# Linear attention into a feed-forward layer: stepping the state every 64 tokens, with block-diagonal k^T and scaled q^T from one crossbar transpose

## The chip, the cores and the metric

One core of one Trainium2 chip runs the whole program. The metric is device time in microseconds (us), one launch, median over several executions. Each execution carries a state. "Slow" means here that it took over 1.5% longer than the fastest of the same kernel; verdicts use the fast ones. Engine names: TensorE (PE in profiles; PEld is its weight load), VectorE (DVE), ScalarE (ACT), GpSimd (POOL), SyncE (SP; its DMA queue is SPq). In the text, "crossbar transpose" is a DMA transpose from on-chip memory to on-chip memory, and "software queue" is the DMA queue that GpSimd issues.

## The reference

Linear attention with a decay per head (4 sequences, 8 heads, 768 tokens, head size 64), then a feed-forward layer of 512 to 2048 to 512 over the 3072 tokens:

```python
for b in range(nb):                      # blocks of 64 tokens
    intra = einsum('bhic,bhjc->bhij', qb, kb) * Dmask      # lam^(i-j), i >= j
    intra = einsum('bhij,bhjd->bhid', intra, vb)
    inter = einsum('bhid,bhde->bhie', qb * lam_pow, kv_state)
    out[:, :, sl] = intra + inter
    kv_state = lam_block * kv_state + einsum('bhsd,bhse->bhde', kb * rev_pow, vb)
...
h = x @ w_in
g = where(h >= 1, h, where(h <= -1, 0, (h + 1)**2 / 4))    # SmeLU
return g @ w_out
```

Inputs and output are float32; the kernel computes in bfloat16 with float32 sums.

## The kernel before

It works in chunks of 128 tokens, 24 in all, 6 per sequence. The decays are moved into tables: v is multiplied by lam^-n, q by lam^n, so no mask with powers is needed and the state is a plain sum. All engines run from one static plan: a small planner in the kernel gives every operation an assumed duration and orders each engine's instructions by it. An engine executes its list in that order.

Chunks 0 to 3 ("plain") transpose k and q on TensorE. From chunk 4 on, k^T lies block-diagonally (two heads on 128 partitions), in two halves g of 64 tokens; the queries of the first half meet only the first half's keys, those of the second half meet both:

```python
def f_xt(c):                              # from chunk 8: crossbar; chunks 4 to 7 use TensorE
    nc.sync.dma_start_transpose(out=t..., in_=qk[c]...)          # 8 blocks of 128x128: k and q
def cast_v(c):
    nc.gpsimd.tensor_tensor(vn, qkv_ld[c, 2], tab_k, op=mult)    # one multiply, 128x512
def f_vb(c, g, hi):                       # 4 small copies per chunk, by DMA, into block-diagonal v
    nc.gpsimd.dma_start(out=vi[HD[hi], :, g, hi, :], in_=vn[HD[g], :, hi, :])
def f_kb(c, hi):                          # block-diagonal k^T, two DVE copies
    nc.vector.tensor_copy(kbd[HD[hi], :, :, hi, :], ptt[c][HD[hi], 0]...)
def f_qT(c):
    nc.vector.tensor_tensor(qT[c], ptt[c][:, 1], tab_q, op=mult)
def f_u(c):                               # state update, 4 matmuls of 128 columns per chunk
    ...
def f_s(c, g):                            # scores: 4 of 128 columns (g=0), 4 of 64 (g=1)
    nc.tensor.matmul(pst[c, g][:, hp, :], lhsT=kbd[:, hp, g], rhs=qT[c][:, hp, 64 * g:])
def f_o(c):                               # output: per pair of heads, state then values
    for hp in range(HP):
        nc.tensor.matmul(po[:, hp], lhsT=ubd[...], rhs=qT[c][:, hp, :])               # 128 columns
        for g in range(2):
            nc.tensor.matmul(po[:, hp, 64 * g:], lhsT=vi[:, hp, g], rhs=sc_sb[c][g])  # 128, 64
# ... feed-forward: L1 into ph, ACT relu -> r, DVE t, w, gT, L2 into py
```

The feed-forward work of DVE is three operations per group: t = min(r/2, 1), w = r - t, gT = w * t, 48 of each.

## Time and profile before

| | before |
|---|---|
| time, median of 3 (range) | 221.22 us (220.75 to 221.24) |
| span of the profiled execution | 220.2 us |
| busy: TensorE, DVE, ACT, GpSimd | 96%, 70%, 62%, 47% |
| first second-layer matmul starts | 35.9 us |
| last weight block landed | 48.1 us |

A busy share says only that an engine had something to do.

### The profile page before, as it was taken

To read this page: it belongs to the slowest core of one execution; us is meant where nothing else is said; L and a number is where in the kernel's file an instruction comes from. 1 tells how busy PE (TensorE), PEld (TensorE's weight loads), DVE (VectorE), ACT (ScalarE), POOL (GpSimd) and SP (SyncE) were. 2 spreads that over 40 slices of the span, in tenths; PEclk is the share of its full clock that TensorE was granted. 3 is DMA by queue.
4 is the path that set the end of the run, shared out by engine and by line. 5 is a ranking of instruction groups with operands and counts; after the bars stand their busy time and mean duration, and the time that the engine had idled before them with its cause. 6 is when DMAs were issued, how large, how long until landed. Compare 5 with 4: busy or idle time off the path is not lost.

```text
span 220.2 us, 5365 instructions
## 1 busy us (share of the span) xinstructions
PE 210.5 (96%) x2147; PEld 152.2 (69%) x2180; DVE 154.8 (70%) x276; ACT 136.2 (62%) x249; POOL 103.7 (47%) x143
## 2 busy tenths in 40 slices
PE   7897999989999999999999999999999999999993
PEld 2566788866787858978877677767677776766441
DVE  6543888999499695998999887687668657364200
ACT  6766685655689558677867667755755753554121
POOL 8999874972588545746664357336060000000000
PEclk9999999999999999999999999999999999999999
DMA  5999999959999999989878895796533110110112
GB/s 139 237 239 234 264 209 233 191 98 249 252 245 206 254 226 272 196 223 228 166 186 210 208 209 141 185 212 166 148 75 99 48 47 3 48 48 33 67 57 86
DMA packets 83945, 36.54 MB, mean 166 GB/s; under 512 B 74256, under 2 KB 78352, under 8 KB 83920
## 3 DMA queue, kind: packets, MB, share of 16 engines
q1 hardware_dynamic: 75472, 24.39, 47.6%
q0 software_dynamic: 8304, 11.80, 23.8%
q8 instruction: 17, 0.28, 0.5%
q14 instruction: 8, 0.07, 0.1%
q10 hardware_dynamic: 144, 0.00, 0.0%
HBM read 27.27 MB, written 6.29 MB: 152 GB/s over the span
## 4 chain that ended last, share of the span: by engine, by line
PE 81%; DVE 8%; POOL 5%; DMA 4%; issue 1%; ACT 0%; POOLq 0%; ACTq 0%
PE py L386 35%; PE ph L347 34%; DMA w_in_sb<-in_moe_w_in_dram 4%; PE ps L306 3%; PE po L330 3%; DVE w L365 2%; PE po L324 2%; PE pu L294 2%; DVE gT L380 2%; DVE t L361 2%; POOL x2f L428 1%; POOL vn L262 1%; PE pt L275 1%; DVE sc L317 1%; POOL x1f L428 1%
## 5 line engine op out<-in xcount | busy, mean ns | idle before, releaser
L347 PE MATMUL ph<-xT,w_in_sb 128*128 128x128 bf16 (+1 forms) x1152 | 98.9, 237 | 1.1 <-DMA w_in_sb<-in_moe_w_in_dram 1.1
L355 ACT ACTIVATE r<-ph,one 128x512 bf16<-128x512 f32 x96 | 65.6, 687 | 53.0 <-PE ph L347 41.1
L386 PE MATMUL py<-w_out_sb,gT 128*128 128x512 bf16 x354 | 90.0, 379 | 1.5
L347 PEld LDWEIGHTS <-w_in_sb 128*128 128x128 bf16 x1152 | 80.5, 98 | 12.4 <-DMA w_in_sb<-in_moe_w_in_dram 1.3
L386 PEld LDWEIGHTS <-gT 128*128 128x128 bf16 x384 | 35.8, 98 | 28.7
L269 POOL DMA_DIRECT2D vi<-vn x80 | 50.2, 644 | 10.2 <-POOL vn L262 6.2
L262 POOL TENSOR_TENSOR vn<-x2f,tab_k 128x512 bf16<-128x512 f32 x24 | 27.4, 1140 | 46.0 <-DMA x2f<-in_v_dram 33.2
L361 DVE TENSOR_SCALAR t<-r 128x1024 bf16<-128x1024 bf16 x48 | 27.5, 572 | 28.6 <-ACT r L355 28.6
L365 DVE TENSOR_TENSOR w<-r,t 128x1024 bf16<-128x1024 bf16 x48 | 36.9, 769 | 1.2
L380 DVE TENSOR_TENSOR gT<-w,t 128x1024 bf16<-128x1024 bf16 x48 | 35.3, 735 | 0.9
L317 DVE TENSOR_TENSOR sc<-ps,causal 128x512 bf16<-128x512 f32 (+1 forms) x40 | 22.1, 553 | 5.7 <-PE ps L306 5.4
L391 ACT COPY osb<-py 128x512 f32<-128x512 f32 x24 | 14.1, 586 | 13.9 <-PE py L386 13.1
L337 ACT CAST xT<-po 128x512 bf16<-128x512 f32 x24 | 14.0, 584 | 9.1 <-PE po L330 7.6
L298 ACT CAST ubd<-pu 64x256 bf16<-64x256 f32 x40 | 14.6, 364 | 1.6 <-PE pu L294 1.4
L306 PEld LDWEIGHTS <-kbd 128*128 128x128 bf16 x160 | 10.8, 98 | 6.9 <-issue 0.9
L252 ACT CAST qk<-x0f 128x512 bf16<-128x512 f32 x23 | 14.1, 615 | 0.7 <-DMA x0f<-in_q_dram 0.6
L306 PE MATMUL ps<-qT,kbd 128*128 128x128 bf16 (+1 forms) x160 | 13.3, 206 | 1.0 <-DVE qT L288 0.8
L252 ACT CAST qk<-x1f 128x512 bf16<-128x512 f32 x23 | 14.1, 613 | 0.0
L324 PE MATMUL po<-qT,ubd 128*128 128x128 bf16 x80 | 13.6, 221 | 0.0
L330 PE MATMUL po<-sc,vi 128*128 128x128 bf16 (+1 forms) x160 | 12.9, 206 | 0.0
L229 PE MATMUL py<-idle 128*128 128x512 bf16 x33 | 10.8, 464 | 1.5 <-DVE one L117 1.2
L330 PEld LDWEIGHTS <-vi 128*128 128x128 bf16 x160 | 11.1, 98 | 1.4
(50 smaller groups left out, 122.9 us busy)
## 6 DMA issues: line engine op xcount, KB each, us to landing
out_dram<-osb SPq DMA_DIRECT2D x24, 256.0 KB, 2.2
x1f<-in_k_dram SPq DMA_DIRECT2D x18, 256.0 KB, 3.8
x0f<-in_q_dram SPq DMA_DIRECT2D x18, 256.0 KB, 4.2
x2f<-in_v_dram SPq DMA_DIRECT2D x17, 256.0 KB, 4.5
vi<-vn POOLq DMA_DIRECT2D x80, 32.0 KB, 3.6
w_in_sb<-in_moe_w_in_dram POOLq DMA_DIRECT2D x4, 512.0 KB, 8.3
w_out_sb<-in_moe_w_out_dram POOLq DMA_DIRECT2D x4, 512.0 KB, 9.5
x2f<-in_v_dram POOLq DMA_DIRECT2D x7, 256.0 KB, 4.9
```

Source lines behind the costliest of these rows:

```text
L252: nc.scalar.copy(out=t, in_=qkv_ld[c, x])
L262: nc.gpsimd.tensor_tensor(vn[c % NV].rearrange("p a b d -> p (a b) d"), qkv_ld[c, 2], _bc(tab_k[:, c % NCB, :], 2, D), op=AX.mult)
L269: (nc.gpsimd if c < VP else nc.sync).dma_start(out=o, in_=i)
L306: nc.tensor.matmul(pst[c, g][:, hp, :], lhsT=kbd[c % NKB][:, hp, g].rearrange("p a d -> p (a d)"), rhs=qT[c][:, hp, 64 * g:], start=True, ...
L317: nc.vector.tensor_tensor(sc_sb[c][g], pst[c, g], _bc(causal[:, 0:128 - 64 * g], 1, HP), op=AX.mult)
L330: nc.tensor.matmul(po[:, hp, 64 * g:], lhsT=vi[c % NV][:, hp, g].rearrange("p a d -> p (a d)"), rhs=sc_sb[c][g][:, hp, :], start=(cb == 0 ...
L347: nc.tensor.matmul(ph[:, j * m:(j + 1) * m], lhsT=w_in_sb[:, ko, (i + j) * 128:(i + j + 1) * 128], rhs=xT[s][:, ko, p * m:(p + 1) * m], st ...
L355: nc.scalar.activation(out=r_t[grp][:, i, :], in_=ph_t[s, ni, part], func=AF.Relu, bias=one[:, 0:1])
L361: nc.vector.tensor_scalar(t_t[grp], r_t[grp], 0.5, 1.0, op0=AX.mult, op1=AX.min)
L365: nc.vector.tensor_tensor(w_t[grp], r_t[grp], t_t[grp], op=AX.subtract)
L380: nc.vector.tensor_tensor(o, w, t, op=AX.mult)
L386: nc.tensor.matmul(py_t[s, ms], lhsT=gT[s][:, ko, ms * 128:(ms + 1) * 128], rhs=w_out_sb[:, ko, :], start=(ko == 0), stop=(ko == FO - 1))
```

## The change

Its intent: make chunks of 64 tokens, from chunk 4 on, out of each 128. Then no query meets another half's keys, scores and values need only 64-column matmuls, and the state steps in between. The block structure is made before the transpose: four casts of k, each of a quarter (64 partitions, 256 elements), write to other partitions than they read and lay k block-diagonally; q is scaled in its cast; one crossbar transpose of 12 blocks then yields both. TensorE's transposes of chunks 4 to 7 go. The DMA copies of v become GpSimd operations: four quarter multiplies and two copies per chunk. In chunks 1 to 3 the order of the output matmuls changes.

```diff
+    LD, RING, VBN, VCN = 6, 6, 620, 600       # planner's durations of the new GpSimd work
+    KE = ('ACT', 'DVE', 'ACT', 'DVE')         # engines of the four k casts
+    def f_ki(c, g, hi):
+        o, i = kq[c % NKQ][HD[hi], HP * g:HP * g + HP, HD[hi]], quarter(qkv_ld[c, 1], g, hi)
+        if KE[2 * g + hi] == "ACT":
+            nc.scalar.copy(out=o, in_=i)
+        else:
+            nc.vector.tensor_tensor(o, i, i, op=AX.max)
+    def f_qn(c):
+        nc.vector.tensor_tensor(kq[c % NKQ][:, 2 * HP:, :]..., qkv_ld[c, 0], tab_n..., op=AX.mult)
     def f_xt(c):
-        ...  in_=qk[c]                        # 8 blocks, chunks 8 to 23
+        nc.sync.dma_start_transpose(out=t, in_=kq[c % NKQ]...)     # 12 blocks, chunks 4 to 23
+    # cast_v, from chunk 4: four quarters with another output partition
+            nc.gpsimd.tensor_tensor(vn[c % NV][HD[hi], HP * g:HP * g + HP, :], quarter(qkv_ld[c, 2], g, hi), ...)
-        (nc.gpsimd if c < VP else nc.sync).dma_start(out=o, in_=i)
+        nc.gpsimd.tensor_copy(vi[c % NV][HD[hi], :, HD[hi]], vn[c % NV][HD[hi]])
     def f_s(c, g):                            # 8 matmuls of 64 columns per chunk
+                for j in range(2):
+                    nc.tensor.matmul(t[:, hp, HD[j]], lhsT=kT[c][:, HP * j + hp, :], rhs=qT[c][:, hp, HD[j]], ...)
     def f_o(c):
+        if c < PLAIN:                         # chunks 0 to 3: the state matmuls first, then the values
+            ...
+        for j in range(2):
+            for hp in range(HP):
+                if cb > 0 or j > 0:
+                    nc.tensor.matmul(po[:, hp, HD[j]], lhsT=ubd[(2 * c + j - 1) % NUB][:, hp, :], rhs=qT[c][:, hp, HD[j]], ...)
+                nc.tensor.matmul(po[:, hp, HD[j]], lhsT=vi[c % NV][:, HP * j + hp, :], rhs=sc_sb[c, 1][:, hp, HD[j]], ...)
 # ... buffers, loads (chunk 6 to the SyncE queue), planner entries cut
```

## The prediction

> **What bounds the kernel now.** I read the page's busy table and slices first, then the chain that ended last, then TensorE's timeline, and last the DVE and GpSimd timelines where TensorE stood still.
>
> ```profile
> span 220.2 us, 5365 instructions
> ...
> PE 210.5 (96%) x2147; PEld 152.2 (69%) x2180; DVE 154.8 (70%) x276; ACT 136.2 (62%) x249; POOL 103.7 (47%) x143
> ...
> PE   7897999989999999999999999999999999999993
> ...
> PEclk9999999999999999999999999999999999999999
> ...
> PE 81%; DVE 8%; POOL 5%; DMA 4%; issue 1%; ACT 0%; POOLq 0%; ACTq 0%
> ```
>
> The fourth line is the busy share of TensorE in 40 slices of 5.5 us: below 9 only in the first four slices, in slice 9 (44 to 49.5 us), and at the end. The clock is full. 81% of the last chain (last line) is TensorE. But busy time is not peak, so I checked the spacing of starts:
>
> ```profile
> 111.85 0.28 PE L306 MATMUL ps<-qT,kbd 128*128 128x64 bf16 x4
> 111.97 1.04 PE L347 MATMUL ph<-xT,w_in_sb 128*128 128x256 bf16 x8
> 112.84 0.39 PE L294 MATMUL pu<-vn,qk 128*128 128x128 bf16 x4
> 113.07 1.03 PE L386 MATMUL py<-w_out_sb,gT 128*128 128x512 bf16 x4
> 113.93 0.22 PE L324 MATMUL po<-qT,ubd 128*128 128x128 bf16 x1
> 113.98 0.25 PE L330 MATMUL po<-sc,vi 128*128 128x128 bf16 x2
> ...
> 114.49 1.04 PE L347 MATMUL ph<-xT,w_in_sb 128*128 128x256 bf16 x8
> ```
>
> Each row is start, duration, what, how many; a group lasts until the next group's start. Four 64-column matmuls take 0.12 us (30 ns each), eight of 256 columns 0.87 (109 ns), four of 512 0.86 (215 ns), and four triples of 128, 128 and 64 columns (113.93 to 114.49) 0.56, so 56 + 56 + 28 ns. Nothing stands between them. So from about 34 us the time is a sum over columns: a matmul removed there comes off the end, if nothing else stalls. The one large stall is this, and the two rows after it (DVE) tell why:
>
> ```profile
> 48.81 0.38 PE L306 MATMUL ps<-qT,kbd 128*128 128x128 bf16 x4 [0.84 <-DVE qT L288]
> ...
> 40.01 1.83 DVE L361 TENSOR_SCALAR t<-r 128x1024 bf16<-128x1024 bf16 x1
> ...
> 43.66 2.35 DVE L365 TENSOR_TENSOR w<-r,t 128x1024 bf16<-128x1024 bf16 x1
> ```
>
> These DVE operations otherwise take 0.42 and 0.69 us. GpSimd's multiply for v ran at 40.47 and 44.39 us, within both.
>
> **What the Trainium skill says.** (1) "TensorE: Matmul & The Clock Gate", section "Wait — 56ns, not 53.3ns?": start to start N/2.4 GHz plus about 2.5 ns, 55.6 ns at 128 columns, with a floor of about 25 ns. For 64 columns that makes 29 ns, above the floor; the trace agrees (30 and 56). (2) The same page, "Back-to-back issue gap", gives about 81 ns at 128 columns in a real stream with weight loads; the trace does not agree (56 ns, with a load before each), and I take the trace. This matters: if weight loads bound, splitting 128 columns into two 64s would gain nothing. (3) "SBUF — State Buffer", section "SBUF: two separate sides": GpSimd and VectorE share a port pair, locked for a whole instruction, when DVE runs a two-port mode or has two SBUF inputs. The 1.83 and 2.35 us above agree. (4) "DMA: Bandwidth & Descriptors", "DMA Transpose (X-bar)", lets the transpose run from the Sync queue only in 2-byte types; the trace has 16 of them there. No figure is taken from it.
>
> **The change, part by part.** Counts are from the instruction lists of the two builds; prices 29 ns (64 columns) and 56 ns (128). TensorE, chunks 4 to 23:
>
> - PE transposes of chunks 4 to 7 go to the crossbar: 32 x 56 = -1.79 us.
> - Scores: 80 of 128 and 80 of 64 (6.80 us) become 160 of 64 (4.64): -2.16. The block-diagonal k of 64 tokens only meets its own 64 queries.
> - Scores times v, the same counts: -2.16.
> - State times q: 68 of 128 (3.81) become 148 of 64 (4.29), since also the first block of a sequence has a half with a past: +0.48.
> - State update: 64 of 128 (3.58) become 12 of 128 and 132 of 64 (4.50): +0.92, as the state also steps in mid chunk.
>
> Sum -4.71 us. All of it lies after 34 us, on the path.
>
> In chunks 1 to 3 the output matmuls are reordered: state matmuls first, then the half-width ones, where before they alternated. Alternating is dear: in chunk 3, starts run from 32.06 to 33.41 us, 1.35 us for 12 matmuls, while chunk 0, with eight half-width ones alone, needs 0.35. After: 4 x 56 + 350 + about 100 for one switch = 0.67. So -0.7 per chunk. Chunk 3 is on the path; chunk 2 gates the next first-layer group through its eviction, so I count it too; chunk 1 is swallowed by the wait for the second weight block (1.12 us at 19.63). One more filler matmul is planned after chunk 3: +0.2. Net -1.2.
>
> TensorE in all: -4.7 - 1.2 = -5.9 us.
>
> Other engines, by these rows (count, busy us, mean ns, idle):
>
> ```profile
> L269 POOL DMA_DIRECT2D vi<-vn x80 | 50.2, 644 | 10.2 <-POOL vn L262 6.2 <-issue 2.0 <-PE po L330 1.0
> L262 POOL TENSOR_TENSOR vn<-x2f,tab_k 128x512 bf16<-128x512 f32 x24 | 27.4, 1140 | 46.0 <-DMA x2f<-in_v_dram 33.2 <-PE ph L347 6.4 <-PE ps L306 6.4
> L298 ACT CAST ubd<-pu 64x256 bf16<-64x256 f32 x40 | 14.6, 364 | 1.6 <-PE pu L294 1.4
> L252 ACT CAST qk<-x0f 128x512 bf16<-128x512 f32 x23 | 14.1, 615 | 0.7 <-DMA x0f<-in_q_dram 0.6
> L288 DVE TENSOR_TENSOR qT<-xq,tab_q 128x512 bf16<-128x512 bf16 x16 | 11.3, 705 | 0.4
> L281 DVE COPY kbd<-xq 64x512 bf16<-64x512 bf16 x32 | 9.8, 305 | 0.2
> ```
>
> DVE per chunk loses two kbd copies (0.61), qT (0.70) and the half mask (0.42) = 1.73, and gains one q scaling (about 0.69, as the 512-element fp32 casts of chunk 0 took) and two quarter casts (estimate 0.42 each, as the 256-element mask from PSUM) = 1.53: -0.2 each, -4 in all. ACT loses 40 casts (24.6 us), gains 40 quarter casts and 40 state evictions at 364 ns (29.1): +4.5 on 136, with slack. GpSimd loses 80 DMA issues (51.5) and 20 full multiplies (22.8); it gains 80 quarter multiplies and 40 copies. At about 0.6 us each (an estimate: half the full multiply; the 512-element memsets took 0.57) that is 72 against 74: equal busy time, but its real SBUF work grows from 23 to 72 us in those chunks, and that is what takes DVE's lock. Today twenty-odd multiplies cost DVE about 13 us (the sum of what t, w and gT took above 0.42, 0.69, 0.69 when one overlapped). Shorter instructions cost less per collision, but there are more: my estimate is another 10 us of DVE. Net DVE 155 - 4 + 10 = about 161 of 216 us, still short of full on average, but tight at 40 to 50 us, where it is 98% busy now.
>
> DMA: twenty transposes of 12 blocks replace sixteen of 8. One held the Sync queue 1.24 us (at 111.50), so about 1.9 each: 38 us against 20, less the 8.7 us (mean over 16 engines) of the vi copies now gone. Spread over 180 us this is hidden.
>
> **Rivals.** (a) The gain is hidden: DVE, locked out by GpSimd, becomes the bound in the first third and TensorE waits for gT or for free r buffers. For: the two long DVE rows, the 0.84 us wait. Against: after 120 us DVE is at 70 to 80% and the gain there stays; DVE also loses work. It would cost 1 to 4 us: 217 to 220. (b) The last w_out block comes too late: now it lands at about 48 us, and second-layer groups are pulled ahead of chunk 4's output, so it is wanted at about 44. Against: its issue moves up too, because chunk 6 no longer loads ahead of it on that queue. Up to 2 us: 217 to 218. (c) Weight loads bind in long runs of 64 columns: 620 matmuls at 40 ns instead of 29 give back 6 us: 222. Against: runs of four at 30 ns each show no slowing by the fourth. (d) All goes well and the 0.84 us stall and the second wait for the split mask go too: 214.
>
> **Range and chances.** 221.2 - 5.9 = 215.3; I add 0.6 for (a) and (b) together: 215.9. 8 in 10: 213.8 to 218.4. The 2% line is 216.8, 0.9 us above my figure and 1.5 above the clean sum, so faster 0.64, same 0.33, slower 0.03.
>
> **What would show it.** Right: 64-column matmuls still 28 to 30 ns apart in runs of eight and sixteen; no L275-type transposes after chunk 3; TensorE's sum of starts from the fifth first-layer group to the end shorter by about 4.5 us; stalls after 34 us no more than 1.5 us. Wrong: DVE t operations of over 1 us more often than today's handful with TensorE idle behind DVE; TensorE waiting at 43 to 47 us for w_out; a transpose's landing named ahead of the scores; 64-column matmuls over 35 ns apart.

## The result, and the profile after

| | before | after |
|---|---|---|
| first rounds, median (range) | 220.99 us (220.47 to 221.24) | 231.08 us (227.42 to 308.46) |
| ratio of fast runs, 95% interval | | 1.0342 (1.0253 to 1.0431) |

Slower, and outside the range. A ratio is always the mean time of one kernel's fast runs over that of the other's of the same rounds, so it is not quite the ratio of the medians quoted. The one execution of 308.46 us ran at a granted clock of 0.657, and it was the profiled one. I therefore ran the changed kernel again (the first experiment, e0) and read its fast profile: first its page.

```profile
span 230.2 us, 5683 instructions
...
PE 209.3 (91%) x2312; PEld 147.8 (64%) x2312; DVE 173.4 (75%) x257; ACT 142.0 (62%) x286; POOL 124.8 (54%) x160
...
PE   7889999179999998699987999997999999999993
...
PEclk9999999859999999999999999999999999999999
...
PE 54%; DVE 27%; DMA 10%; issue 4%; POOL 2%; ACT 1%; ACTq 0%; POOLq 0%
```

TensorE's share of the last chain fell from 81% to 54%, and DVE and DMA hold the rest. One slice of TensorE's 40 (5.75 us each) has 1 tenth: that is 40 to 46 us. In that slice and the next the granted clock falls to 8 and 5 tenths. Later, five more slices are under 9, between 86 and 161 us. So there are two kinds of hole, and the timeline of the same run shows one of each (columns as in the prediction; SPq is SyncE's DMA queue):

```profile
32.24 4.65 SPq L273 DMA_TRANSPOSE xq<-kq  x1
...
40.12 1.03 PE L407 MATMUL py<-w_out_sb,gT 128*128 128x512 bf16 x4
47.23 0.61 PE L324 MATMUL ps<-xq 128*128 128x64 bf16 x8 [6.08 <-DMA xq<-kq]
...
95.88 0.19 PE L349 MATMUL po<-xq,ubd 128*128 128x64 bf16 x1
97.69 0.19 PE L351 MATMUL po<-sc,vi 128*128 128x64 bf16 x1 [1.61 <-DVE sc L331]
...
94.81 1.47 DVE L264 TENSOR_TENSOR kq<-x1f 64x256 bf16<-64x256 f32 x2
96.31 0.73 DVE L382 TENSOR_SCALAR t<-r 128x1024 bf16<-128x1024 bf16 x1
96.95 0.68 DVE L331 TENSOR_TENSOR sc<-ps,causal 128x512 bf16<-128x512 f32 x1
...
94.29 1.71 POOL L284 COPY vi<-vn 64x512 bf16<-64x512 bf16 x2
96.06 3.68 POOL L281 TENSOR_TENSOR vn<-x2f,tab_k 64x256 bf16<-64x256 f32 x4
```

**The early hole.** Chunk 4's transpose is issued at 32.24 us, holds its queue for 4.65 us, and lands only when the scores can start, at 47.2 us. TensorE stands still 6.25 us (counted from start to start of the matmuls, less the column time of the first), and after it runs for a while at half clock: 512-column matmuls follow at 426 instead of 216 ns, which costs about 1.45 us more.

**The late holes.** At 95.88 us the output group of a chunk stops because the masked scores (sc) are not there. DVE was not idle: the two casts of k for a later chunk, and a t, stand in its list ahead of the mask. The casts take 1.47 us instead of the 0.75 that the planner assumed, and GpSimd is busy beside them without a pause. Nine such holes between 77 and 160 us sum to 9.75 us.

The groups of the same profile (busy us and mean ns) show the sizes that I had to guess:

```profile
L281 POOL TENSOR_TENSOR vn<-x2f,tab_k 64x256 bf16<-64x256 f32 x80 | 63.3, 791 | 50.3 <-DMA x2f<-in_v_dram 37.8
...
L386 DVE TENSOR_TENSOR w<-r,t 128x1024 bf16<-128x1024 bf16 x48 | 39.8, 829 | 1.3
L401 DVE TENSOR_TENSOR gT<-w,t 128x1024 bf16<-128x1024 bf16 x48 | 39.3, 818 | 1.5
L284 POOL COPY vi<-vn 64x512 bf16<-64x512 bf16 x40 | 33.6, 840 | 2.1
...
L264 DVE TENSOR_TENSOR kq<-x1f 64x256 bf16<-64x256 f32 x40 | 25.4, 636 | 1.0
...
L267 DVE TENSOR_TENSOR kq<-x0f,tab_n 128x512 bf16<-128x512 f32 x20 | 18.1, 904 | 0.3
```

The same page of before has for w and gT:

```profile
L365 DVE TENSOR_TENSOR w<-r,t 128x1024 bf16<-128x1024 bf16 x48 | 36.9, 769 | 1.2
L380 DVE TENSOR_TENSOR gT<-w,t 128x1024 bf16<-128x1024 bf16 x48 | 35.3, 735 | 0.9
```

The k casts took 636 ns (predicted 420), q's scaling 904 (690), GpSimd's quarter multiply 791 and copy 840 (600 each).

The sum for this profile: columns saved -4.6, early hole +6.25, half clock +1.45, late holes +9.75, together +12.85 us, where the spans differ by +10.0. The difference is roughly what stands at the start, where the second layer begins at 33.5 us instead of 35.9, and before's own wait of 1.0 us at 47.6 us, which is gone.

The theory at this point had two causes. A: DVE, lengthened by GpSimd and given casts on the way, delivers masks late. B: the first crossbar transpose runs inside the stream of weights and is slow there, and delays what it runs beside. Rivals: a third cost of the new step itself (64-column matmuls, evictions on ACT); and a bad order, planned with too short durations.

### The profile page after: what moved, and what is told of

Read it like the earlier page. It is cut to its first block, busy times and chain, and to the rows that moved or that the text cites. A ratio compares the mean times of both kernels' runs of the same rounds, so it can differ in the third digit from the quotient of the medians.

```text
span 306.2 us, 5683 instructions
## 1 busy us (share of the span) xinstructions
PE 300.2 (98%) x2312; PEld 191.3 (62%) x2312; DVE 163.4 (53%) x257; ACT 143.8 (47%) x286; POOL 116.7 (38%) x160
## 4 chain that ended last, share of the span: by engine, by line
PE 96%; POOL 2%; issue 0%; ACT 0%; POOLq 0%; ACTq 0%
PE py L407 41%; PE ph L368 41%; PE py L232 3%; PE pu L312 3%; PE ps L324 2%; PE po L351 2%; PE po L349 2%; PE ps L321 1%; PE pt L290 1%; POOL x2f L450 1%; PE po L343 1%; POOL vn L278 0%; PE po L339 0%; POOL x1f L450 0%; POOL x0f L450 0%
## 5 line engine op out<-in xcount | busy, mean ns | idle before, releaser
L368 PE MATMUL ph<-xT,w_in_sb 128*128 128x128 bf16 (+1 forms) x1152 | 140.2, 292 | 0.0
L407 PE MATMUL py<-w_out_sb,gT 128*128 128x512 bf16 x384 | 137.7, 514 | 0.0
L368 PEld LDWEIGHTS <-w_in_sb 128*128 128x128 bf16 x1152 | 106.6, 118 | 29.5 <-issue 15.5
L281 POOL TENSOR_TENSOR vn<-x2f,tab_k 64x256 bf16<-64x256 f32 x80 | 58.4, 730 | 88.1 <-DMA x2f<-in_v_dram 77.4
L284 POOL COPY vi<-vn 64x512 bf16<-64x512 bf16 x40 | 30.4, 759 | 16.2 <-PE po L351 14.4
L315 ACT CAST ubd<-pu 64x256 bf16<-64x256 f32 x80 | 29.1, 363 | 14.5 <-PE pu L312 10.5
L264 DVE TENSOR_TENSOR kq<-x1f 64x256 bf16<-64x256 f32 x40 | 22.2, 554 | 1.0
L358 ACT CAST xT<-po 128x512 bf16<-128x512 f32 x24 | 14.0, 585 | 14.5 <-PE po L351 9.3
L262 ACT CAST kq<-x1f 64x256 bf16<-64x256 f32 x40 | 16.0, 401 | 0.4
L267 DVE TENSOR_TENSOR kq<-x0f,tab_n 128x512 bf16<-128x512 f32 x20 | 15.4, 769 | 0.3
L351 PE MATMUL po<-sc,vi 128*128 128x64 bf16 x160 | 15.5, 217 | 0.0
L349 PE MATMUL po<-xq,ubd 128*128 128x64 bf16 x148 | 14.9, 217 | 0.0
L349 PEld LDWEIGHTS <-ubd 128*128 128x128 bf16 x148 | 12.9, 111 | 2.8 <-issue 2.7
```

The source lines that it names most:

```text
L281: nc.gpsimd.tensor_tensor(vn[c % NV][HD[hi], HP * g:HP * g + HP, :], quarter(qkv_ld[c, 2], g, hi), _bc(tab, 2, D), op=AX.mult)
L284: nc.gpsimd.tensor_copy(vi[c % NV][HD[hi], :, HD[hi]], vn[c % NV][HD[hi]])
L315: nc.scalar.copy(out=ubd[(2 * c + j) % NUB][HD[hi], :, HD[hi]], in_=pu[0][HD[hi], :, HD[hi] if c < NCB else HD[0]])
L349: nc.tensor.matmul(po[:, hp, HD[j]], lhsT=ubd[(2 * c + j - 1) % NUB][:, hp, :], rhs=qT[c][:, hp, HD[j]], start=True, stop=False)
L351: nc.tensor.matmul(po[:, hp, HD[j]], lhsT=vi[c % NV][:, HP * j + hp, :], rhs=sc_sb[c, 1][:, hp, HD[j]], start=(cb == 0 and j == 0), stop=True)
L368: nc.tensor.matmul(ph[:, j * m:(j + 1) * m], lhsT=w_in_sb[:, ko, (i + j) * 128:(i + j + 1) * 128], rhs=xT[s][:, ko, p * m:(p + 1) * m], st ...
```

## The experiments

All ran with three timed rounds. Every run but e7 gave the correct result. Times are medians with the range; before was 221.2 to 222.1 us in every set of rounds.

**e0: the changed kernel again.**

> The changed kernel unaltered, because the only profile of it so far fell on an execution with the TensorE clock at 0.65, in which TensorE is the bound by force and no stall shows. Theory A (GpSimd's instructions lock VectorE out; VectorE is late with gT or the mask, TensorE waits): at full clock 225 to 232 us, with TensorE busy under 92% and 8 us or more of TensorE idle time put down to DVE or to work behind DVE; t, w, gT means above 0.55, 0.77, 0.75 us. Theory B (a chain latency: crossbar transpose or the loads in front of it land too late): the same time, but the waits name a DMA or the chain kq, xq, ps. Theory C (the kernel itself draws the clock down): the time is 215 to 218 whenever the granted clock is 1.000, and the clock is below 0.99 in most executions of this kernel while the kernel before stays at 1.000.

Measured: 231.99 us (229.34 to 233.51), ratio 1.0401 (1.0314 to 1.0489). The slowdown is no matter of the slow state. Its lines are those above.

**e1: the new step from chunk 6 instead of 4** (no crossbar while weights come in).

```diff
-    PLAIN, KA = 4, 1
+    PLAIN, KA = 6, 1
```

> The changed kernel, with the new scheme from chunk 6 instead of chunk 4 (chunks 4 and 5 are transposed on TensorE as chunks 0 to 3 are). In the changed kernel's profile TensorE idles 6.2 us at 40.8 us on the crossbar transpose of chunk 4, which took 14.9 us from issue to landing (median 4.0), and then runs some 7 us at half clock. Theory B (the early transpose is the loss): that stall and the half clock go, at a price of about 1.8 us for the extra TensorE work: 224 to 227 us. Theory A alone (VectorE locked out by GpSimd, nine stalls of 9.8 us in all at the output matmuls behind the mask): these stay, so with A and B both true 224 to 227; if the early stall was only covering a VectorE backlog, no gain: 229 to 232.

Measured: 230.40 us (229.23 to 231.10), ratio 1.0401. The early hole is gone: the slowest transpose landed in 5.1 us, and the last weights at 41.1 instead of 47.6 us. But a new hole of 4.4 us stands at 61 us behind the mask, and five others of 0.6 to 1.8 us. Mending B alone returns 1.6 us by the medians, and nothing by the ratio, which is that of e0: the holes behind the mask, 9.75 us in e0, sum to 10.7 us here.

**e2: all four k casts on ACT.**

```diff
-    KE = ('ACT', 'DVE', 'ACT', 'DVE')
+    KE = ('ACT', 'ACT', 'ACT', 'ACT')
```

> The changed kernel with all four quarter casts of k on ACT, none on VectorE: 40 casts of 636 ns leave VectorE (25 us), 40 of about 400 come to ACT (16 us). Theory A: the stalls of the output matmuls behind the mask (9.8 us) fall below 4 us, the early stall (theory B) stays: 223 to 227 us. If these stalls come from ACT or from the order of the plan, no gain or a loss: 229 to 233.

Measured: 224.69 us (222.48 to 225.90), ratio 1.0111 (1.0019 to 1.0204). DVE fell from 173.4 to 148.8 us busy; of the late holes one of 0.4 us is left, beside 1.1 us before a second-layer group at 63 us, which waits for ACT's eviction (osb), itself behind four k casts on ACT. The early hole (5.5 us, landing 15.6 us) and its half clock stay. So A is the larger part, and it can be mended apart from B.

**e3: the copies of v on ACT instead of GpSimd**, to see what GpSimd costs DVE.

```diff
-        nc.gpsimd.tensor_copy(vi[c % NV][HD[hi], :, HD[hi]], vn[c % NV][HD[hi]])
+        nc.scalar.copy(out=vi[c % NV][HD[hi], :, HD[hi]], in_=vn[c % NV][HD[hi]])
# ... the planner's entry, moved to ACT, cut
```

> The changed kernel with the block-diagonal copies of v on ACT instead of GpSimd: GpSimd loses 40 copies of 840 ns (33.6 us of 125), VectorE's own instructions are the same in number and shape. Theory A (the lock between the two): VectorE's w, gT, kq and q-scaling means fall (829, 818, 636 and 904 ns before) by a third or more of their excess over 690, 690, 425 and 690, its busy time falls by 6 to 10 us, and stalls of 3 to 6 us go: 225 to 228 us. If VectorE is slow for another reason (partition shifts, strides), its means stay and the time is 229 to 233.

Measured: 232.92 us (230.69 to 233.30), ratio 1.0495. No gain in time, but a clean reading: with the same DVE instructions DVE took 159.9 us instead of 173.4 (k cast 525 ns, q scaling 795, w 773, gT 758). What GpSimd does lengthens what DVE does. The time went to ACT, 164.4 us busy, whose late r kept the first layer waiting, and the early hole was 7.7 us.

**e4: the kernel before with crossbar transposes already from chunk 4**, nothing else of the change.

```diff
-    NQK, NXT, XT = 4, 2, 8
+    NQK, NXT, XT = 4, 2, 4
```

> The kernel before with crossbar transposes from chunk 4 instead of chunk 8 and nothing else: 32 TensorE transposes fewer (1.8 us). Theory B1 (any crossbar transpose at 32 to 45 us, while the weights stream in on the other queue, is slow): the first transposes take 8 us or more to land and TensorE stalls 2 to 6 us there: 221 to 226 us. Theory B2 (it is slow because it has 12 blocks, or because of what else the change moved): they land in 4 to 6 us and the time is 219 to 220.5.

Measured: 226.87 us (225.96 to 227.59), ratio 1.0241 (1.0181 to 1.0301). It has 32 TensorE transposes less, 1.8 us of columns, and is 5.5 us slower (226.87 against 221.37). The transpose of only 8 blocks landed in up to 10.6 us, where before had 6.2, and holes of 0.9, 1.4 and 1.3 us with a half-clock stretch stand at 44 to 49 us. This is B, without the casts and GpSimd work of A; its cost stands in the time, its path only in part in the trace. No hole names a transpose: the first two end with the mask, the third with a multiply of v on GpSimd, which had waited 2.1 us for a load before the multiply ahead of it. DVE itself waited 1.1 and 3.5 us for transposes. The last line of the view by tile in e0, in e4 and in e5 (the next run):

```profile
DMA to landing us min/median/max: 3.2/4.0/14.9
```

```profile
DMA to landing us min/median/max: 2.7/4.0/10.6
```

```profile
DMA to landing us min/median/max: 3.2/3.6/6.0
```

The medians are alike; only the early ones are slow.

**e5: both repairs**, chunk 6 and all k casts on ACT.

```diff
-    PLAIN, KA = 4, 1
+    PLAIN, KA = 6, 1
-    KE = ('ACT', 'DVE', 'ACT', 'DVE')
+    KE = ('ACT', 'ACT', 'ACT', 'ACT')
```

> Edit: the changed kernel with both repairs at once: the new step starts at chunk 6, and all four k casts are on ACT. Theory (two separate causes, the first crossbar transpose inside the weight stream and the vector engine lengthened by GpSimd): each repair alone took away its own stalls, so together the output stalls should be under 2 us in sum, the crossbar's landing at most 6 us, no half clock after 40 us, and the time 216 to 219 us. Rival (the kernels differ for a third reason, the matmul order or the extra evacuations on ACT): it stays at 221 to 225 us although both kinds of stall are gone, and ACT, which gets about 4 us more casts, shows waits of the first layer on r. A second rival: starting at chunk 6 shifts all of the new step's work to a place where the vector engine is full, as in the run with chunk 6 alone (4.4 us stall at 61 us); then the stall there stays above 3 us.

Measured: 218.52 us (218.19 to 218.93), ratio 0.9877 (0.9855 to 0.9900). This version beats both kernels. Its page:

```profile
span 216.6 us, 5668 instructions
...
PE 208.5 (96%) x2312; PEld 147.6 (68%) x2312; DVE 149.8 (69%) x221; ACT 155.9 (72%) x322; POOL 120.7 (56%) x150
...
PE   7889998999999999999999999999999999999992
...
PEclk9999999999999999999999999999999999999999
...
PE 73%; DVE 16%; POOL 5%; DMA 4%; issue 1%; ACT 1%; POOLq 0%; ACTq 0%
```

No slice of TensorE after the first 40 us is under 9 until the end, and the clock is full. The gains show that A and B hide each other: by the medians chunk 6 alone returned 1.6 us, the casts alone 7.3, both 13.5 (by the ratios, e0's 1.0401 became 1.0401, 1.0111 and 0.9877). The rival of a third cost falls: with both causes gone, the new step's own sum comes out (for 18 chunks, at the prediction's prices: transposes -0.9, scores -1.7, values -1.7, state times q +0.5, update +0.5, so -3.3 us; the span is 2.9 us shorter than that of e8, which is before in all but an order).

**e6: e2 with the first transpose held back until the last weights have landed.**

```diff
+        if c == PLAIN:
+            tc.add_manual_dep(d.ins, w_dma[7].ins.name, SYNC)
# ... the same dependence in the planner's entry cut
```

> Edit: the run with all k casts on ACT, and the first crossbar transpose (chunk 4) issued only after the last weight load has landed. Theory (the transpose is slow only because the weight stream runs beside it, and the stream's end is delayed by it): the transpose issued at about 41 us lands in 4 to 5 us, at about 46 us instead of 47; the last weight load lands at about 41 us instead of 47.6; w_out no longer delays the second layer. The stall before chunk 4's scores stays at 3 to 6 us because the scores are asked for at 41 us, so the time is 222 to 225 us, against 224.7. Rival (the transpose's own volume is slow, whoever runs beside it): its landing stays above 8 us and the time rises to 227 us or more.

Measured: 224.62 us (223.81 to 225.51), ratio 1.0145; level with e2. The transposes are quick when nothing streams (at most 5.6 us), so it is not their own volume, and the rival falls. But the rest of the expectation was missed: the last weights landed at 45.5 us although no transpose ran beside them, with the load issued by GpSimd only at 37.5 us, behind its own multiplies of v; the transpose was issued only at 49.1 us, behind seven loads. By the time, waiting for the stream costs as much as running in it, but the holes are others: 1.8 us for the weights at 44 us, and six behind the mask, 4.2 us in sum, although no k cast is left on DVE.

**e7: GpSimd's copies of v left out from chunk 8 on** (a wrong result).

```diff
-        for hi in range(0 if P else 2):
+        for hi in range(0 if P or c >= PLAIN + NV else 2):
```

> Edit: the changed kernel without GpSimd's two copies of v into the block-diagonal tiles from chunk 8 on (wrong result on purpose: old v in the blocks); everything else as in the changed kernel. It takes some 32 GpSimd copies away and moves no work to another engine. Theory (GpSimd's instructions lengthen the vector engine's): DVE busy falls by 8 to 14 us with the same instructions, the stalls at the output matmuls after 75 us fall from 9.8 us to under 4 us, and the time falls to 224 to 228 us; the first stall of 6 us at 41 us and its half clock stay. Rival (the stalls come from the vector engine's own added instructions, two k casts and a scaled cast of q per chunk, not from the lock): DVE busy falls by less than 4 us and the time stays at 230 to 232 us.

Measured: 224.86 us (222.29 to 227.41), two of four executions slow; fast ratio 1.0081. DVE fell by 6.7 us, less than the 8 to 14 expected, and the holes at the output matmuls after 50 us summed to 5.8 us, not under 4. In between theory and rival: the lock is a part of A, and DVE's own new work is another. In the fast profile the early hole, which I had expected to stay at 6 us, was only 2.0 us and behind the mask: the transpose had landed in 8.1 us, before TensorE came to its scores. So of the 9.7 us between the spans of e0 and e7, more than half is the early hole and its half clock, which vary from execution to execution.

**e8: the kernel before with only the new order of the output matmuls in chunks 1 to 3.**

```diff
+        if c < PLAIN:
+            # four state matmuls, then the eight of the values
```

> Edit: the kernel before with one thing of the change, the order of the output matmuls of chunks 1 to 3 (the four state matmuls first, then the eight of the values). The prediction gave this 1.2 us of the gain. Theory of the prediction: 219.5 to 220.4 us. Rival (the time goes to idle or filler matmuls that nothing waits for): 220.8 to 221.4 us, ratio within 0.2%.

Measured: 221.42 us (220.41 to 224.03), ratio 0.9992 (0.9960 to 1.0025). Nothing, where the prediction counted 1.2 us (a ratio of 0.9946, outside the interval). The groups did become as short as the prediction said (0.66 us for chunk 3, where it was 1.35), and in the two profiles chunk 4's scores start at 48.07 us instead of 48.81. But TensorE waits 1.4 and 0.6 us for weights at 14 and 20 us, where before waited 1.1 us once, and 1.18 us instead of 1.01 before chunk 4's scores. The plan has 36 fillers (idle matmuls that nothing waits for) in both kernels, counted by their weight loads.

**e9: the changed kernel with measured durations in the planner.** No work changes, only the order on the engines.

```diff
-    LD, RING, VBN, VCN = 6, 6, 620, 600
+    LD, RING, VBN, VCN = 6, 6, 850, 800
-  ("ki", ...) 375          ("qn", ...) 690
+  ("ki", ...) 640 on DVE, 400 on ACT     ("qn", ...) 900
```

> Edit: the changed kernel with the durations that its planner assumes for the added work set to those measured (GpSimd's quarter multiply 800 ns instead of 600 and copy 850 instead of 620, k casts 640 on the vector engine and 400 on ACT instead of 375, the scaled cast of q 900 instead of 690). No work is added or taken away, only the order on the engines moves. Theory (the loss is contention: the transpose in the weight stream, and the vector engine's real load): the time stays at 228 to 233 us and vector-engine busy time within 4 us of 173. Rival (the loss is a bad order, made with too short durations): the output stalls fall to under 3 us and the time to 220 to 224 us.

Measured: 225.09 us (223.79 to 229.39), ratio 1.0119 (1.0052 to 1.0187). This was a miss of mine: I had given the order little, and it returns about 7 us.

**e10: e5 with the measured durations.**

> Edit: the version with both repairs (new step from chunk 6, all k casts on ACT) with the measured durations in the planner. TensorE already stands at 96% there, so both theories expect little: 217.5 to 219.5 us; below 217.5 us would say that the plan still cost something.

Measured: 218.34 us (217.71 to 219.86), ratio 0.9845 (0.979 to 0.990). As expected: where TensorE is dense, the durations do nothing. It is level with e5.

**e11: e2 from chunk 5** (`PLAIN = 5`, all k casts on ACT).

> Edit: all k casts on ACT, and the new step from chunk 5 instead of 4 or 6. Theory (the first crossbar transpose costs what it overlaps of the weight stream): one chunk later than chunk 4 is issued at about 40 us, at or after the last weights land (41 to 43 us), so its landing stays under 8 us and the time is 217 to 220 us; by TensorE's columns alone it would be 0.6 us under the version from chunk 6. Rival (what matters is how much of the new work falls before 55 us, whatever the weights do): halfway between the versions from chunk 4 and 6, 221 to 222 us.

Measured: 220.22 us (218.56 to 220.75), ratio 0.9907 (0.9850 to 0.9963). The slowest landing was 6.6 us, as the theory wanted; the time lies at the edge between theory and rival, so the rival (new work before 55 us costs time whatever the weights do) is not excluded.

For the next three, what was open: which holes the durations had closed.

**e12: e9 once more.**

> The changed kernel with the measured durations in the planner once more, for a profile of the fast state. If order on the vector engine was what it mended: output stalls after 70 us under 7 us in sum where the changed kernel had 9.8, and the early wait for chunk 4's transpose still 3 to 6 us. If it was the early wait: that is under 2 us and the output stalls are still 9 to 10 us. Time 223.5 to 226.5 us in either case.

Measured: 223.87 us (222.90 to 227.58), ratio 1.0109. The fast profile fits neither expectation cleanly: the holes at the output matmuls after 60 us sum to 7.4 us instead of 9.75, and the early wait is 0.7 us, behind the mask; the transpose landed in 7.8 us, before TensorE came to its scores. Both fell. How long the early wait is differs between executions: in the profile of e9, the same kernel, the slowest landing was 14.5 us.

**e13: e12 and all k casts on ACT.**

> The same, and all k casts on ACT; new step still from chunk 4. Theory (order and vector-engine load act on the same stalls, the early transpose is separate): output stalls under 2 us, the early wait of 3 to 6 us with its half clock stays, time 221 to 224.5 us, so little below the run with the casts on ACT alone (224.7). Rival (durations mended the early wait): 217 to 219 us.

Measured: 223.53 us (222.51 to 224.17), ratio 1.0102. Of the late holes nothing over 0.3 us is left behind the mask. What stands is 1.1 us before a second-layer group at 46 us, until the last weights landed (46.6 us), 0.5 us before another at 73 us, behind gT, and a wait of 2.2 us for a transpose, with a half-clock stretch after it:

```profile
56.29 2.76 SPq L273 DMA_TRANSPOSE xq<-kq  x1
...
62.51 0.41 PE L324 MATMUL ps<-xq 128*128 128x64 bf16 x8 [2.04 <-DMA xq<-kq]
```

This is chunk 6's transpose, issued ten us after the last weights and landed in 6.2 us, so the wait is not B. The first transpose had the slowest landing, 10.5 us, but no matmul waited for it: the early wait of 3 to 6 us that I had expected is missing. Order and load of DVE act on the same holes: the two repairs together are worth hardly more than one.

**e14: e13 from chunk 5.**

> The same with the new step from chunk 5, whose first transpose is issued as the last weights land. Theory: no half clock, early wait under 2 us, 217.5 to 220 us, level with the versions from chunk 6 (218.3 and 218.5). Rival (the new step costs time wherever it begins before 55 us): 221 us or more.

Measured: 222.14 us (219.04 to 223.38), ratio 0.9966 (0.9877 to 1.0056), two of four slow. The profile has what the theory wanted in DMA (landing at most 5.1 us) and full clock, with a hole of 1.9 us at 51 us behind the mask. The times do not: they spread over 4 us, where e5 spread over 0.7. Why a start at chunk 5 is unsteady stays open.

## Why the prediction was wrong, point by point

**"Sum -4.71 us": right.** The 64-column matmuls stand 29 to 30 ns apart in runs of eight and sixteen, with a weight load each, so rival (c) is out (its 620 matmuls are 600 by the prediction's own counts). Counted from the instruction lists of e8 and e0, idle matmuls left out, at the column formula that the prediction cites, the difference is -4.6 us. It was there to be had, as e5 shows.

**"Net -1.2" for the order in chunks 1 to 3: wrong.** e8 has the order alone and gains nothing. The prediction took a shorter group as a shorter path; the groups shortened, but in that stretch TensorE also waits for weights and for DVE.

**"I add 0.6 for (a) and (b) together": the step that failed.** The late holes cost 9.75 us and the early one 7.7 with its half clock, where 0.6 was allowed. Rival (a) was the right mechanism for the late holes, with two things mis-sized.
- The casts: "two quarter casts (estimate 0.42 each...)" were 0.636, the scaling of q 0.904 instead of 0.69. That is 40 x 0.216 + 20 x 0.214 = 12.9 us, and DVE came to 173.4 us instead of 161. I had priced new DVE instructions as if they ran alone and put the whole lock into a lump of 10 us for the old ones, which grew by only 6.4 us (t, w and gT, 99.7 to 106.1). e3 shows that the casts lengthen with GpSimd like the others.
- GpSimd: "about 0.6 us each" were 0.79 and 0.84, 97 us of memory work instead of 72. All four prices fit the shortest that e0 shows (0.42, 0.68, 0.60 and 0.60 us).

The worse fault was the conclusion "still short of full on average". An in-order engine at 75% delivers late when an urgent operation stands behind two that are not urgent. e12 shows it from the other side, in part: with the order made for the true durations, DVE is even busier (176.1 us), and the late holes fall by 2.4 us. The kernel is 7 to 8 us faster, but most of that difference between the two profiles stands at the early hole. Moving the casts off DVE removed nearly all the late holes in e2 and e13, though not in e6; moving GpSimd's copies to ACT only moved them (e3).

**"Against: its issue moves up too" and "Spread over 180 us this is hidden": wrong.** The transposes are hidden on average (median landing 4.0 us, as fast as the loads). The first is not, because the last weights stream beside it. Between 36 and 43 us the 256-byte packets of the hardware queue (transposes and loads) took 116 ns on average in e0; in e5, 26 ns from 50 to 56 us (with transposes, no weights), and 18 ns from 36 to 41 us (with weights, no transpose). The last weights were issued earlier, as rival (b)'s objection said (34.2 us instead of 39.7), but took 13.7 us instead of 8.7 to land, and so their last packet came at 47.6 us, hardly before the 48.1 of the kernel before. In e1, e5 and e6, with no transpose beside the stream, none took over 6.0 us; in e0 and e4 it was up to 14.9 and 10.6. So it takes both. That the twenty transposes held SyncE's queue for 38.0 us in all, as predicted, was luck: the 1.24 us that the estimate scaled up is the shortest of the sixteen in the kernel before, which held it for 26.5 us and not 20. Of the prediction's own signs of being wrong this one came: a landing named ahead of the scores. By what mechanism the two queues slow each other, no run here shows.

**ACT "+4.5":** 142.0 against 136.2 us, +5.8. Near enough.

**The chances.** I gave "slower" 0.03. A plan that fills TensorE to 96% has no slack in which an engine's new work can be late, and I had seen DVE at 98% in one stretch. That alone called for more.

What stays open: how the 7 us that the order returns divide between the late holes and the early one, as the early one differs between executions of one kernel (0.7 to 5 us); and e14's spread. The granted clock of every execution gives a hint. The half-clock stretch of 6.9 us takes about 0.015 from the mean of e0's profile; three of e0's four executions stand at 0.982 to 0.985, but only one of e9's (0.981, the profiled one) and none of e12's (0.992 and above). So the new order probably made the long early hole rare. It is not the whole loss: e0's fourth execution, at 1.000, still took 229.34 us.

## What to carry to other kernels

Price new instructions by the durations that such instructions have beside their neighbours, not alone, and give the planner those numbers: here that was 7 us with no work changed. Ask where in time a new transfer first runs, not how long it takes on average; a transpose in the middle of the weight stream cost more than all the columns that it saved (e4: 5.5 us slower with 1.8 us of columns less). Two causes that hide each other look weak when mended singly (1.6 and 7.3 us, together 13.5), so run the pair.

## What the Trainium skill lacked or had wrong

- "Advanced Engine Details and Errata", "X-Bar Transpose (TRN2)", says that transposes are as fast as regular DMAs. Away from the weight stream these runs agree (over whole fast profiles, median landing 3.6 to 4.7 us against 3.6 to 4.6 for SyncE's loads of q, k and v). Beside the stream they do not: 10.6 to 15.6 us in e0, e2 and e4, and 8.1 and 7.8 us in e7 and e12. The page has no figure for that.
- "TensorE: Matmul & The Clock Gate", "Back-to-back issue gap": about 81 ns at 128 columns with weight loads. Here it was 56 ns, and 29 to 30 ns at 64 columns; the column formula of "Wait — 56ns, not 53.3ns?" holds.
- The same page, "What's actually happening", puts the half clock after an idle window of about 3.4 us. These runs agree as far as holes of 6.25 us (e0) and 4.4 us (e1) had the clock fall in them or just after, and a hole of 1.9 us (e0) did not. But in e4 holes of 0.9, 1.4 and 1.3 us within 5 us were enough, and in e13 one of 2.2 us.
- "SBUF — State Buffer", "SBUF: two separate sides", describes the lock; the runs agree. It has no figure for what compute on GpSimd costs DVE: 40 GpSimd copies less (33.6 us) took 13.5 us off DVE in e3.
- No page that I used says how much longer GpSimd's own operations take beside a busy DVE: in e0 its multiplies of 64x256 took 0.79 us on average, the shortest 0.60.
